# Mamba-2 scan and GELU layer on one core: the first decay scan widened, Y of two units in Gram banks, and a new hand order

## The chip, the cores and the metric

The kernel runs on one core of one Trainium2 chip. The metric is device time in microseconds, from one launch; the median of three runs stands for the kernel. TensorE (PE), VectorE (DVE), ScalarE (ACT), GpSimd (POOL) and SyncE (SP) each carry out their own instructions in program order and wait for each other through semaphores. SP and ACT also issue DMAs; such an issue holds up what stands behind it on that engine's queue.

## The reference, cut to what matters

```python
# x: (4, 8, 768, 32), a: (4, 8, 768), B and C: (4, 8, 768, 16); chunk-wise decayed linear attention
cum = np.cumsum(log(clip(a)))                  # per chunk
L = exp(cum_i - cum_j) * (i >= j)
M = (C_i . B_j) * L
y = M @ x + exp(cum) * (C @ state)
state = decay_full * state + sum_j decay_from_j * B_j x_j
# the heads are put side by side: 3072 tokens x 256
h = x @ w_in                                   # 256 -> 2048
out = gelu_tanh(h) @ w_out                     # 2048 -> 256
```

All inputs and the output are float32 in HBM; the kernel multiplies in bf16.

## The kernel before

The kernel uses chunks of 128 tokens: six chunks in each of four batches, 24 in all. Two chunks make a unit, so there are 12 units, three in each batch. A step has a name such as `Y.1` (the Y of unit 1) or `s1.0.6` (the first matrix product of unit 0, part 6), and one Python function `f_...` writes its instructions. The order of all steps is written out by hand in the string `ORDERED` (lines 17 to 68). The steps are written in that order, so each engine and each DMA queue works through its own part of it. A suffix `:A`, `:D`, `:P` or `:S` picks the engine for a step that can run on several (its `alt`), `@b` picks the PSUM bank, and `~51` puts in 51 blocks of idle matmuls on a zero tile (line 773).

**The scan.** In place of logarithms, a decay scan runs backwards over each chunk. `Rq` (line 371) scans the first four chunks of batch 0 for all batches' rows (128 partitions by 128); `R` (line 400) scans everything, 128 by 256. `tpq`, `tp2` and `tp6` (line 375) turn the results so that tokens are partitions; `recip0`, `recip1` and `recip` take reciprocals. B is multiplied by the decay (`mulb`, `mul1.0`, `mul.b.0`) and C by its reciprocal (`mulc`, `mul1.1`, `mul.b.1`). Batch 0 is done in two groups: chunks 0 to 3 (`bc0`, `tw`, `ew`) and chunks 4 and 5 (`load_bc1`, `mul1`, `T1`, `ce1`, `bh1`, `N1`, `bn1`). Batch 1 turns its B and C on TensorE (`T`, `E`, `F`, `N`, `bn`). Batches 2 and 3 write the scaled B and C to HBM scratch (`load_wr`, line 521), and read them back, with a DMA transpose (`load_tr`, line 527) and plainly (`load_bn`, line 533). In the names of these steps the last digit is 0 for B and 1 for C: `load_tr.2.0` brings the turned B of batch 2, which `G.6` needs.

```python
            wr = {i: add("S", load_wr, b, i, deps=[mul[i]]) for i in (1, 0)}
            tr = {1: add("S", load_tr, b, 1, deps=[wr[1], after]), 0: add("S", load_tr, b, 0, deps=[wr[0], Gn[last]])}
            bb = add("S", load_bn, b, deps=[wr[0], dn[last]])
...
        if alt:
            s.fn = lambda: fn(*args, {"A": "ACT", "D": "DVE", "P": "POOL", "S": "SP"}[s.eng])
        else:
            s.fn = lambda: fn(*args)
```

These lines (925 to 929 and 834 to 837) show that a `load_wr` step has no `alt`: its function takes no engine and always issues on SP.

**A unit.** `G` makes the Gram blocks in the PSUM tiles `ga` and `gb` (two banks each), `M` masks them into SBUF, `D` makes the state's increment, `S` adds it to the decayed state (line 752), `SP` spreads the state into a masked 128x256 tile (line 759), `Y` multiplies M by x and adds the state's part (lines 701 and 710), and `yev` copies Y to `xm` in SBUF. For units 0 and 1, `XX` and `XD` make x and the increment from one load of x (lines 601 and 611). From unit 4 on, two units are done together (`Yi`, `YI`, `yew`). Y of units 0 to 3 is made in `bank_y`.

**The GELU layer.** `s1` multiplies `xm` by `w_in` into a PSUM bank (lines 790 and 795), `gelu` on ScalarE moves it to SBUF (lines 801 and 804), `s2` multiplies by `w_out` (line 816), `oev` copies the result out of PSUM and `store` writes it. The four banks a, b, o, y are shared by these steps. The weights come as eight 512 KB loads (`load_wi`, `load_wo`) and are cast to bf16 by `wi` and `wo`; x comes by `load_x` (two DMAs for a unit) and is cast by `castx`.

## Time and profile before

| what | value |
| --- | --- |
| median of three runs | 116.5 us (115.69, 116.5, 119.59) |
| the profiled execution's own time | 115.84 us |
| its span, first to last instruction | 114.1 us |
| PE busy | 107.5 us (94%) |
| DVE, ACT, POOL busy | 68.1, 69.7, 24.7 us |
| moved by DMA | 15.99 MB in 43102 packets |
| granted TensorE clock | 1.000 |

The lines of the profile are in the prediction. Busy PE time counts matmuls whose modelled ends overlap, and it counts the idle matmuls on the zero tile too. The span lies 1.7 us below the execution's own time.

### The profile page before, as it was taken

How to read it: one execution, taken by the hardware profiler on the slowest of the kernel's cores; microseconds unless marked ns; L12 is line 12 of the kernel's file. 1: busy time of each engine (PE TensorE's matmuls, PEld its weight loads, DVE VectorE, ACT ScalarE, POOL GpSimd, SP SyncE). 2: the span in 40 equal slices, each digit the busy share in tenths (PEclk: the TensorE clock that was granted, in tenths of full speed). 3: DMA queues.
4: the chain of work that ended last, by engine and by line, in shares of the span. 5: the costliest groups of instructions: out<-in, count | busy, mean ns of one | idle time of the engine just before them, and what ended most of it. 6: DMA issues, size and time to landing. Idle time of an engine off the chain costs nothing.

```text
span 114.1 us, 3122 instructions
## 1 busy us (share of the span) xinstructions
PE 107.5 (94%) x1277; PEld 77.6 (68%) x1285; DVE 68.1 (60%) x136; ACT 69.7 (61%) x135; POOL 24.7 (22%) x53
## 2 busy tenths in 40 slices
PE   6998889999999999999999999999999999999990
PEld 2345566888879888665677765777657776777870
DVE  4789999999989597798509704658444411020110
ACT  3149688687673727479666778725865666654400
POOL 6635676736319000130200200000000000000000
PEclk9999999999999999999999999999999999999999
DMA  0999989989998768968777502220000023201032
GB/s 24 243 303 306 353 222 203 311 151 345 207 215 136 158 163 188 294 128 195 185 161 142 116 0 96 97 92 6 0 0 0 6 91 116 69 0 52 0 138 92
DMA packets 43102, 15.99 MB, mean 140 GB/s; under 512 B 36688, under 2 KB 41552, under 8 KB 43088
## 3 DMA queue, kind: packets, MB, share of 16 engines
q1 hardware_dynamic: 42896, 15.70, 54.9%
q8 instruction: 10, 0.16, 0.7%
q10 hardware_dynamic: 192, 0.09, 0.3%
q14 instruction: 4, 0.03, 0.1%
HBM read 11.07 MB, written 3.93 MB: 131 GB/s over the span
## 4 chain that ended last, share of the span: by engine, by line
PE 78%; SPq 9%; DMA 7%; ACT 1%; issue 1%; POOL 1%; DVE 0%; POOLq 0%
PE bank_o L816 19%; PE bank_y L816 16%; PE bank_b L795 10%; PE bank_a L795 7%; PE bank_b L790 5%; PE bank_a L790 4%; SPq L154 4%; PE bank_o L795 4%; DMA bcf<-in_B_dram 4%; DMA x_t<-in_x_dram 3%; PE bank_y L795 3%; SPq L194 3%; PE bank_b L816 2%; PE bank_a L816 2%; PE ga L637 1%; PE bank_y L721 1%
## 5 line engine op out<-in xcount | busy, mean ns | idle before, releaser
L816 PEld LDWEIGHTS <-gT 128*128 128x128 bf16 x384 | 37.1, 98 | 10.4 <-issue 0.6
L816 PE MATMUL bank_o<-w_out_sb,gT 128*128 128x256 bf16 x192 | 26.1, 273 | 0.0
L816 PE MATMUL bank_y<-w_out_sb,gT 128*128 128x256 bf16 x160 | 21.2, 273 | 0.1
L795 PEld LDWEIGHTS <-w_in_sb 128*128 128x128 bf16 x128 | 14.1, 114 | 7.7 <-issue 0.4
L804 ACT ACTIVATE gT<-bank_b 128x512 bf16<-128x512 f32 x25 | 14.9, 598 | 6.6 <-PE bank_b L795 6.1
L654 DVE TENSOR_TENSOR m<-ga,tri 128x1024 bf16<-128x1024 f32 x12 | 14.6, 1216 | 5.3 <-PE gb L637 5.3
L804 ACT ACTIVATE gT<-bank_a 128x512 bf16<-128x512 f32 x21 | 12.6, 599 | 6.6 <-PE bank_a L795 2.5
L790 PEld LDWEIGHTS <-w_in_sb 128*128 128x128 bf16 x128 | 13.6, 113 | 2.3 <-issue 1.5
L795 PE MATMUL bank_b<-xm,w_in_sb 128*128 128x512 bf16 x48 | 14.5, 380 | 0.2
L801 ACT ACTIVATE gT<-bank_b 128x512 bf16<-128x512 f32 x17 | 10.1, 596 | 6.8 <-PE bank_b L790 6.7
L654 DVE TENSOR_TENSOR m<-gb,tri 128x1024 bf16<-128x1024 f32 x11 | 13.4, 1216 | 0.1
L352 DVE COPY o_sb<-bank_y 128x256 f32<-128x256 f32 x5 | 2.1, 424 | 15.7 <-PE bank_y L816 13.7
L795 PE MATMUL bank_a<-xm,w_in_sb 128*128 128x512 bf16 x36 | 11.2, 380 | 0.1
L801 ACT ACTIVATE gT<-bank_a 128x512 bf16<-128x512 f32 x15 | 8.9, 595 | 2.7 <-PE bank_a L790 2.6
L790 PE MATMUL bank_b<-xm,w_in_sb 128*128 128x256 bf16 x68 | 10.3, 273 | 0.2 <-DVE s_new L752 0.2
L790 PE MATMUL bank_a<-xm,w_in_sb 128*128 128x256 bf16 x60 | 9.0, 272 | 0.9 <-ACT gT L801 0.4
L759 DVE SCALAR_TENSOR_TENSOR sp_new<-s_new,pend,bmask 128x256 bf16<-128x256 f32 x17 | 9.4, 568 | 0.3 <-DVE s_new L752 0.2
L773 PE MATMUL bank_y<-wz 128*128 128x512 bf16 (+2 forms) x21 | 7.6, 512 | 1.1 <-DVE warm L225 1.1
L352 DVE CAST xm<-bank_a 128x512 bf16<-128x512 f32 x4 | 2.8, 692 | 9.0 <-PE bank_a L734 9.0
L804 ACT ACTIVATE gT<-bank_o 128x512 bf16<-128x512 f32 x10 | 6.0, 596 | 2.4 <-PE bank_o L795 2.3
L510 POOL TENSOR_TENSOR bc<-bc_t,pt 128x768 bf16<-128x768 f32 x3 | 4.5, 1494 | 13.0 <-DMA bc_t<-in_C_dram 10.7
L348 ACT ACTIVATE xm<-bank_y 128x512 bf16<-128x512 f32 x8 | 4.8, 594 | 3.6 <-PE bank_a L734 3.1
(149 smaller groups left out, 131.8 us busy)
## 6 DMA issues: line engine op xcount, KB each, us to landing
out_dram<-o_sb SPq DMA_DIRECT2D x24, 128.0 KB, 1.8
x_t<-in_x_dram SPq DMA_DIRECT2D x20, 128.0 KB, 4.3
wf<-in_moe_w_in_dram SPq DMA_DIRECT2D x4, 512.0 KB, 7.6
wf<-in_moe_w_out_dram SPq DMA_DIRECT2D x4, 512.0 KB, 6.0
bc_t<-in_C_dram SPq DMA_DIRECT2D x3, 384.0 KB, 4.7
bc_t<-in_B_dram SPq DMA_DIRECT2D x3, 384.0 KB, 6.0
scr<-bc SPq DMA_DIRECT2D x4, 192.0 KB, 2.7
x_t<-in_x_dram SPq DMA_DIRECT2D x1, 512.0 KB, 4.5
```

The source lines that it names most:

```text
L154: nc.sync.dma_start(out=BC0[1][:, i], in_=(B, C)[i][0, :, c * Q:(c + n) * Q, :] .rearrange("h (p r) n -> p h (r n)", r=n))
L348: nc.scalar.activation(o, i, AF.Copy)
L352: nc.vector.tensor_copy(out=o, in_=i)
L510: (nc.gpsimd if eng == "POOL" else nc.vector).tensor_tensor(out=d["bc16"][:, i], in0=d["bc"].rearrange("p i h (r n) -> p i r h n", r=R6)[: ...
L654: nc.vector.tensor_tensor(out=m_of(u)[:, 2 * i:2 * i + 2].rearrange("p g k e t -> p (g k e) t"), in0=gx[i].rearrange("p g (k t) -> p (g k) ...
L759: nc.vector.scalar_tensor_tensor(out=sp_new.rearrange("p (g d) -> p g d", g=4), in0=(XN[0][:, H * D:H * D + 64] if gc == 0 else state[("s" ...
L773: nc.tensor.matmul(out=t[:, 0:m * 128], lhsT=wz, rhs=w3.to_broadcast([128, m, 128]), start=True, stop=True, skip_group_check=True)
L790: nc.tensor.matmul(out=hp[:, j * T:(j + 1) * T], lhsT=w_in_k[:, w, q, k], rhs=xm[:, w, u * T:(u + 1) * T], start=(w == 0), stop=(w == 1))
L795: nc.tensor.matmul(out=hp, lhsT=w_in_k[:, w, q, k], rhs=xm[:, w, u * T:u * T + PT], start=(w == 0), stop=(w == 1))
L801: nc.scalar.activation(gts[u][:, 2 * i:2 * i + 2], hp.rearrange("p (j t) -> p j t", j=2), AF.Gelu_apprx_tanh)
L804: nc.scalar.activation(gts[("p", u)][:, i], hp, AF.Gelu_apprx_tanh)
L816: nc.tensor.matmul(out=ops[gc], lhsT=gts[u][:, fi, k * Q:(k + 1) * Q], rhs=w_out_sb[:, fi, :], start=(fi == 0 and (u > 0 or k == 0)), stop ...
```

## The change

The diff does six things.

- `load_aq` now loads other rows: for batch 0 the 128 partitions hold chunks 0 to 5, so that the scan `Rq` serves chunks 4 and 5 too. `tp2` goes; `recip1` and `mul1` read what `tpq` made. `peq`, `ppq`, `pendq` and `m4` have six columns.
- `load_bc1` brings B and C of chunks 4 and 5 as 64 partitions with four tokens each (256 B runs) where it brought 128 partitions with two (128 B runs). `mul1`, `T1`, `ce1`, `bh1` follow that shape.
- Y of units 1 and 2 (`YG`) is made in `gb` instead of `bank_y`, its state part with 32x32 tiles, and for these units `SP` writes a 128x64 tile with one operand, on DVE or ACT.
- `pe` can run on POOL; the step `hold.4` goes.
- `XD` now comes before `XX`.
- The order from `mulb` on is another one, with other engines and banks for many steps.

```diff
+    YG = (1, 2)
...
-    BC0 = [const.tile([128, 2, H, n * N], FP32, name=f"bcf{g}") for g, (_, n) in enumerate(GR)]
+    BC0 = [const.tile([P4 * n, 2, H, R4 * N], FP32, name=f"bcf{g}") for g, (_, n) in enumerate(GR)]
...
-                          .rearrange("h (p r) n -> p h (r n)", r=n))
+                          .rearrange("h (p r) n -> p h (r n)", r=R4))
...
+            in_=bass.AP(tensor=a.tensor, offset=a.offset + i * Q, ap=[[R4 * Q, 32 // H], [S, H], [1, Q]]))
...
-    def f_tp2():
-        for k in range(4):
-            q, t = divmod(4 * Q + k * (Q // 2), QL)
-            turn(rt0[1][32 * k:32 * k + 32], r_t[32 * q:32 * q + 32, t:t + Q // 2], 2)
...
     def f_Y(u):
+        if u in YG:
+            for k, w, j in [(k, w, j) for k in range(2) for w in range(2) for j in range(4)]:
+                h = 4 * w + j
+                nc.tensor.matmul(out=gx[1][32 * j:32 * j + 32, w, k * Q:(k + 1) * Q],
+                                 lhsT=X16[u][:, k, 32 * h:32 * h + 32], rhs=MT[u][:, h // 2, k, h % 2],
+                                 start=(k == 0), stop=True, tile_position=(0, 32 * j), skip_group_check=True)
+            for k in range(2):
+                sp = state.pop(("sp", 2 * u + k - 1))
+                for h in range(H):
...
+                    nc.tensor.matmul(out=gx[1][32 * j:32 * j + 32, w, k * Q:(k + 1) * Q],
+                                     lhsT=sp[gs, 32 * e:32 * e + 32], rhs=ce_of(2 * u + k)[gs, e],
+                                     start=False, stop=True, tile_position=(32 * g, 32 * j), skip_group_check=True)
+            return
...
+    def f_SP(gc, eng):
+        if (gc + 1) // 2 in YG:
+            sp_new = st.tile([128, 64], BF16, name="sp_row")
...
-    hold = add("P", f_hold, 4, deps=[SPn[4]])
-    steps["mul.1.1"].deps.append(hold)
```

The new order, in the parts that the prediction speaks of (each line is cut out of the string):

```
recip0 c_m16 mulc.0 ~51 tw.1 ew.1.1:A mulc.1 tw.2 ew.0.1:A c_unp ew.1.2:A ~4 mulb tw.0 load_wi.1 ew.0.0:A
ew.0.2:A c_ends clip R tp6 G.0 peq ~4 ew.1.0:A x4.0:P x4.1:D M.0.0 pe:P GE.3 ppq XD.0 XX.0 ~4 GE.2 ME.3:P
pendq:A ME.2:D xn.1:A xn.0:D wi.0.0:A SP.0 S.0.0 S.0.1 load_wi.2 load_wi.3 Y.0 load_bc1.1 G.1 yev.0.0.2:A
...
load_bc1.0 wi.1.0:P gelu.0.0 wi.2.0:D SP.2:D wi.1.1:P s1.0.2@o s1.0.3@y gelu.0.2 wi.2.1:P s1.0.4@b
gelu.0.4 s1.0.5@o wi.3.0:P M.1.0 mul1.1:P Y.1 pp@a load_wo.0 gelu.0.3 load_x.2:S wi.3.1:D mul1.0:D
s1.0.6@y yev.1.0.2:A recip.1 gelu.0.5 gelu.0.6 T1.0 T1.1 wo.0.0:P bh1:D load_wo.2 s1.0.7@b N1 s1.1.0@y
...
D.4@a load_x.5:S SP.6 Y.3 s2.1.0.2 s2.1.0.3 castx.5.None:P load_wr.2.1:S load_x.6:A oev.2:A S.4.0
load_x.7:S yev.3.0.2:D S.4.1 SP.9 load_tr.2.1 s1.3.0@y s1.3.1@b s1.3.2@a gelu.3.0 gelu.3.2 s1.3.3@o
load_wr.2.0:A s2.1.1.0@y s2.1.1.1 M.4.1 s2.1.1.2 gelu.3.1 M.4.0 G.5 D.5@b S.5.0 gelu.3.3 s2.1.1.3 oev.3:A
SP.7 s1.3.4@b s1.3.5@o s1.3.6@a gelu.3.6 gelu.3.5 load_bn.2 SP.10 M.5.0 M.5.1 gelu.3.4 s2.2.0.0@y
load_tr.2.0 s2.2.0.1 F.2 s2.2.0.2 castx.6.None:D s2.2.0.3 oev.4:D s1.3.7@a castx.7.None:P gelu.3.7 SP.8
s2.2.1.0@o s2.2.1.1 s2.2.1.2 Yi.4@ya Yi.5 YI.4 YI.5 G.6 D.6@b D.7@y load_bc.3.0 s2.2.1.3 load_x.11:A
```

Before, the same stretch on SP's queue was: `load_x.5 load_x.6 load_wr.2.1 load_x.7 load_wr.2.0 load_tr.2.1 load_bn.2 load_tr.2.0`.

## The prediction

> **What bounds the kernel now.** I read first the page's head and its slices: how full TensorE is, and where it is not.

> ```profile
> span 114.1 us, 3122 instructions
> PE 107.5 (94%) x1277; PEld 77.6 (68%) x1285; DVE 68.1 (60%) x136; ACT 69.7 (61%) x135; POOL 24.7 (22%) x53
> ...
> PE   6998889999999999999999999999999999999990
> ...
> DMA  0999989989998768968777502220000023201032
> ```

> TensorE is full from the seventh slice (about 17 us) to the end; only the start has room, and there the DMA engines are full for the first 13 slices (37 us). Next the stages, by a view of four windows, cut at the points that the chain of waits gave below (us busy and instructions for PE, PEld, DVE, ACT and POOL; then clock, DMA share and GB/s).

> ```profile
> 12.40:20.35 7.95, 6.83 (x92) 5.15 (x93) 7.84 (x21) 6.39 (x13) 5.95 (x11) 1.00 0.99 242
> 20.35:31.50 11.15, 11.15 (x148) 9.75 (x148) 10.60 (x17) 7.98 (x15) 5.78 (x9) 1.00 0.99 253
> 31.50:45.60 14.10, 13.95 (x198) 11.96 (x201) 11.43 (x20) 8.07 (x17) 3.49 (x3) 1.00 0.83 171
> 45.60:111.10 65.50, 65.01 (x700) 45.70 (x708) 28.98 (x50) 40.50 (x79) 2.72 (x3) 1.00 0.34 87
> ```

> From 20.35 us on TensorE is busy 11.15 of 11.15, 13.95 of 14.10 and 65.01 of 65.50 us. In these stages nothing can be won but about 0.6 us; time can only be lost. In the first it is busy 6.83 of 7.95 us, and real idle time is more, since the modelled ends of matmuls overlap: nine `s1` steps at the 0.44 us that four matmuls take when nothing waits (eight take 0.89 in the chain below), and about 1.6 us of small work, leave some 2.3 us. DVE is busy 7.84 of 7.95 us there, and the DMA engines are at 0.99. The chain of waits says where that stage ends:

> ```profile
> 19.68 0.62 POOL x L350
> 20.35 0.21 PE bank_b L679 x4
> ...
> 31.47 0.89 PE bank_o L816 x8
> ```

> Until 20.35 the chain runs through the cast of x for unit 2 on POOL and `D.2`, which waits for it; from there it is TensorE alone. The step that ends at 32.36 (31.47 + 0.89) is `s2.0.1.3`. The changed order has done exactly the same `s1` and `s2` parts and units when it ends that step, so I use it as a milestone. The timeline shows the pace ahead of it:

> ```profile
> 8.83 1.20 DVE L654 TENSOR_TENSOR m<-ga,tri 128x1024 bf16<-128x1024 f32 x1
> ...
> 11.59 0.58 ACT L348 ACTIVATE xm<-bank_y 128x512 bf16<-128x512 f32 x1
> ...
> 15.04 1.17 POOL L350 CAST w_in_sb<-wf 128x512 bf16<-128x512 f32 x2 [0.20 <-DMA wf<-in_moe_w_in_dram]
> ...
> 15.59 0.60 ACT L801 ACTIVATE gT<-bank_a 128x512 bf16<-128x512 f32 x1 [0.20 <-PE bank_a L790]
> ...
> 16.72 0.60 PE L790 MATMUL bank_b<-xm,w_in_sb 128*128 128x256 bf16 x4
> 16.77 0.68 POOL L470 TENSOR_TENSOR bc0s<-bcf,rt 128x256 bf16<-128x256 f32 x1 [0.56 <-DMA bcf<-in_B_dram]
> ...
> 16.87 0.60 ACT L801 ACTIVATE gT<-bank_a 128x512 bf16<-128x512 f32 x1 [0.20 <-PE bank_a L790]
> ...
> 17.36 0.59 ACT L801 ACTIVATE gT<-bank_b 128x512 bf16<-128x512 f32 x1
> ...
> 18.76 0.60 PE L790 MATMUL bank_b<-xm,w_in_sb 128*128 128x256 bf16 x4
> ```

> `M.0.0` starts at 8.83, Y of unit 0 is copied at 11.59. The `s1` steps of unit 0 go round two banks, so each waits for the `gelu` two steps ahead: the `gelu` of bank a start 1.28 us apart (15.59, 16.87), 0.64 for one, while ScalarE can start one each 0.49 us (16.87, 17.36). `s1.0.6` is the row at 16.72. Then `s1.0.7` comes only at 18.76, since `T1`, `Y.1`, `pp` and `N1` stand in front of it and wait for B of chunks 4 and 5. The POOL rows show two landings, since both had waited for a DMA: `w_in` part 3 at 15.0, B of chunks 4 and 5 at 16.7.

> **The change part by part, the start.** The prices come from groups of instructions by shape (busy us and mean ns):

> ```profile
> L375 DVE STREAM_TRANSPOSE rt<-r_t 32x64 f32<-32x64 f32 x4 | 0.9, 238 | 0.1
> L362 DVE TENSOR_SCALAR ac<-a_t 128x256 f32<-128x256 f32 x1 | 0.3, 283 | 0.0
> L365 DVE TENSOR_TENSOR_SCAN r_t<-ac,ends 128x256 f32<-128x256 f32 x1 | 0.7, 692 | 0.1
> L375 DVE STREAM_TRANSPOSE rt<-r_t 128x192 f32<-128x192 f32 x1 | 0.5, 519 | 0.0
> L451 DVE TENSOR_TENSOR bc0s<-bcf,rt 128x512 bf16<-128x512 f32 x1 | 0.7, 691 | 0.4 <-DMA bcf<-in_B_dram 0.4
> L510 DVE TENSOR_TENSOR bc<-bc_t,rt 128x768 bf16<-128x768 f32 x2 | 1.9, 952 | 0.0
> L510 POOL TENSOR_TENSOR bc<-bc_t,rt 128x768 bf16<-128x768 f32 x1 | 1.7, 1681 | 0.0
> L759 DVE SCALAR_TENSOR_TENSOR sp_new<-s_new,pend,bmask 128x256 bf16<-128x256 f32 x17 | 9.4, 568 | 0.3 <-DVE s_new L752 0.2
> ```

> *Decay.* `tp2` goes (0.9 us of DVE) and `pe` goes to POOL. But `clip`, `R` and `tp6` (0.28, 0.69 and 0.52 us) now stand ahead of `M.0.0` on DVE; most of that lies in the wait for `G.0` and x. All six `ew` copies are on ACT, where DVE had two, so one more stands ahead of `G.0`: between 0 and the 0.58 us of the copy at 11.59, which is twice as wide; I take 0.3. With `ME.2` on DVE, Y of unit 0 is copied at about 12.0 rather than 11.59: **+0.4 us**.

> *`mul1` on half the partitions* is 512 elements wide instead of 256. On DVE that is the 0.69 us of `mulb` (line 451). On POOL, 256 elements took 0.68 and 768 took 1.68, so 1.1 to 1.2. They lie beside the `s1` steps of unit 0; if uncovered they cost 0.4 us each. The 64-column `SP` has a quarter of the elements of the 568 ns row, and takes between 0.14 and 0.57 us; I take 0.25. That frees 1.2 us of DVE or moves it to ACT, in a stage in which DVE is full. `load_bc1` has half as many packets. The two old loads took 1.7 us (15.0 to 16.7); the saving lies between 0 and half of that, I take 0.5 us for all later loads.

> *Y of units 1 and 2 in `gb`* has 32 matmuls of 128 columns as before: 0.45 us if four run side by side, as their column positions allow (eight of 256 columns take 0.89 in a row), and 1.1 if the new state part did not. I take no change, since TensorE has idle time around `Y.1`. Its worth is that `bank_y` is free: the `s1` steps of unit 0 go round three banks, so the pace is that of ScalarE, 0.5 us, not 0.64. Over the seven steps up to `Y.1` that is **-1.0 us**; it can't be more, because `w_in` part 3 lands at 15.0 whatever the order. `Y.1` stands ahead of `s1.0.6`, so the hole before `s1.0.7` shrinks by **0.4 us**. `s1.0.7` then starts at 17.8.

> *Up to the milestone.* `D.2` stands after four parts of unit 1, so it no longer waits for x (about 0.5 us of the time up to 20.35): **-0.5**. Against it, `mul.1.0` takes 1.68 us on POOL instead of 0.95 on DVE, behind a bc load that comes later by one weight load (512 KB at 253 GB/s is 2 us): `T.1.0` makes TensorE wait **+0.3**. Three `w_out` casts and `E.1.0` on ACT lie in the time that ACT has spare (it is busy 7.98 of 11.15 us).

> Sum: +0.4 - 1.0 - 0.4 - 0.5 + 0.3 = **-1.2 us** at the milestone. Bounds: -3.0 if TensorE had no hole at all after 12.4, +0.4 if only the later start stays.

> **The change, where the lead goes.** After the milestone the work on TensorE is the same, so the lead is kept only if nothing that comes by DMA is late. I followed SP's queue (start and length of each issue), one POOL row, and the landing times of the scratch transfers (min, median, max) and of the transposes:

> ```profile
> 26.54 2.71 SPq L168 DMA_DIRECT2D bc_t<-in_C_dram  x1
> ...
> 35.73 0.67 SPq L524 DMA_DIRECT2D scr<-bc  x1
> 36.45 2.26 SPq L175 DMA_DIRECT2D x_t<-in_x_dram  x2
> 38.81 0.89 SPq L524 DMA_DIRECT2D scr<-bc  x1
> 40.13 1.23 SPq L531 DMA_TRANSPOSE ch<-scr  x1
> 41.59 0.39 SPq L536 DMA_DIRECT2D bn<-scr  x1
> 42.03 1.23 SPq L531 DMA_TRANSPOSE bh<-scr  x1
> ```

> ```profile
> 34.15 1.49 POOL L510 TENSOR_TENSOR bc<-bc_t,pt 128x768 bf16<-128x768 f32 x1 [2.29 <-DVE s_new L752]
> ```

> ```profile
> DMA to landing us min/median/max: 2.1/2.8/4.4
> ```

> ```profile
> bh<-scr SPq DMA_TRANSPOSE x2, 3.1
> ```

> ```profile
> 45.60 0.29 PE L637 MATMUL ga<-ce,bh 32*64 32x256 bf16 x1
> ```

> Here `L510` at 34.15 is `mul.2.1`: its bc load, issued at 26.54, landed just then. It ends at 35.64, and SP writes C to scratch at 35.73. SP goes on to x for unit 7 and writes B to scratch at 38.81. At 40.13, when the first write has landed (4.4 us, the maximum), it issues C's transpose; at 41.59, when the second has landed, the plain reload; and at 42.03 B's transpose, which lands 3.1 us later at about 45.2. `G.6` (line 637) needs that and starts at 45.60, right behind `YI` on TensorE. So the old order met that load with 0.4 us to spare, and a lead of 1.2 us brings TensorE there 0.8 us too early, if the load comes as before.

> The new order moves `load_x.6` off SP to ACT, and puts the write of B behind the transpose of C. The mark `load_wr.2.0:A` changes nothing, because that step has no choice of engine and issues on SP. So: `mul.2.1` ends at 35.1 (35.64 less the 0.5 from `load_bc1`). The write lands between 2.1 and 4.4 us later. It now has only one unit's x ahead of it on SP's queue instead of two, so I take the 2.7 of the old second write: 37.8. C's transpose holds SP for 1.23: 39.1. Then B's write, again 2.7: 41.85; the reload is issued with 0.05 to spare, and B's transpose 0.44 after it, as before: 42.35, landed 45.45. **`G.6` starts at 45.5 instead of 45.60: -0.1 us is left of the lead**, and TensorE stands idle for 1.1 us ahead of it. `D.6`, `D.7`, `s2.2.1.3` and all later parts queue behind `G.6`.

> [...]

> **ACT's DMA issues.** `load_x.6`, `.11` and `.10` on ACT are two issues each: 0.8 us by the unhindered 0.39 at 41.59, and up to 2.3 us by the SP row of `load_x.7` (36.45). They stand where ACT waits for TensorE anyway (ACT is busy 8.07 of 14.10 us). I take 0; uncovered, about 1 us.

> **Batch 3** has the same pattern: `load_wr.3.0` holds up SP ahead of `load_bc.3.1`. Its transposes are needed by `G.9`, and by the same steps I count some 6 us to spare. I take 0.

> Sum against the execution's own time: 115.84 - 0.1 = **115.7 us**; the median shown is 0.7 above that execution.

> **The rivals.**

> *The lead is kept.* If B's write lands at the minimum of 2.1 us, and C's at 2.1 too, G.6's load lands at 44.2, and TensorE, which arrives at 44.4, does not wait: 115.84 - 1.2 = 114.6 us, and down to 113.0 if the start comes near its bound of -3.0. For it: fewer packets, and one unit's x less on SP's queue. Against it: the DMA share of 0.83 up to 45.6, and landings of 2.7 to 4.4 in just that stretch.

> *Slower, by the order on SP.* If either write lands in 4.4 us, as the old one did, B's transpose is 1.7 us later, lands at 47.15, and `G.6` starts at 47.2 rather than 45.60: 115.84 + 1.6 = 117.4. It decides as soon as B's transpose is issued after 42.4. For it: nothing overlaps any more, C's write, C's transpose and B's write follow one another. Against it: SP's queue is less full by then.

> *The change doesn't do what it says at the start.* Products on POOL slow DVE, and there is no lead.

> ```profile
> 34.19 1.73 DVE L759 SCALAR_TENSOR_TENSOR sp_new<-s_new,pend,bmask 128x256 bf16<-128x256 f32 x1
> ```

> This `SP` took 1.73 us while POOL multiplied, against 0.57 in the mean: 1.2 us for one instruction. If that strikes at `F.1`, which `G.3` needs, the lead is 0. TensorE then reaches `G.6` at 45.6, its load is there, and the time is 115.84 to 116.3, I take 116.0. [...]

> **How the numbers follow.** Lead spent at `G.6`, 115.7 us: 0.43 (own range 115.0 to 116.4). Lead kept, 114.6: 0.28. Slower on SP, 117.4: 0.16. No lead, 116.0: 0.13. The range of 8 in 10 goes from 114.0 to 117.6: it takes in both landing bounds and leaves out a start that gains over 1.8 us and a stall of over 1.8. The chances go by 2%, about what a measurement of this kernel can tell from no change: below 114.2 (of 116.5) lies about half of "lead kept", the half with the better start, 0.15; above 118.8 lies the part of "slower" that has a second stall, for `G.9` or for x, and a little of the unforeseen, 0.10; the rest, 0.75, is within 2%.

> **What would show it.** Right: `s2.0.1.3` ends near 31.2, the issue of B's transpose of batch 2 lies near 42.4 and behind C's, `G.6` at 45.5 has idle time before it of about 1 us, and TensorE is full from there. Wrong: `G.6` without idle time and earlier than 45 (lead kept), `G.6` at 47 (slower), or `s2.0.1.3` at 32 or later (no lead). What would make it wrong altogether is a hole of TensorE after 46 us, or a start in which the first `s1` step of unit 0 comes after 13.5.

## The result, and the profile after

The changed kernel takes **119.7 us** (median of 119.11, 119.48, 119.87 and 122.64), the kernel before 116.4 in the same series. The ratio is 1.029, with a 95% interval of 1.023 to 1.035: slower, where 115.7 us within 114.0 to 117.6 had been forecast. The profiled execution took 119.87 us, with a span of 118.2 instead of 114.1. (The ratio leaves disturbed executions out, here 122.64 and one of 119.59 of the kernel before; so do the medians and ratios below, by which the changed kernel takes 119.5.)

The page's head and slices, to be held against those of before:

```profile
span 118.2 us, 3112 instructions
PE 110.8 (94%) x1276; PEld 77.9 (66%) x1284; DVE 67.5 (57%) x132; ACT 69.2 (59%) x136; POOL 25.9 (22%) x52
...
PE   6977699999999999999999999999999999999990
...
PEclk9999755999999999999999999999999999999999
```

TensorE has 3.3 us more busy time with one instruction less, and the clock row has a dent in its fifth to seventh slice (12 to 21 us) that the kernel before does not have. The stages again, cut at the steps of this kernel (PE, PEld, DVE, ACT, POOL busy; then clock, DMA share, GB/s):

```profile
13.50:20.00 6.50, 6.50 (x75) 3.99 (x72) 5.39 (x14) 3.28 (x8) 3.74 (x6) 0.50 1.07 239
...
20.50:35.50 15.00, 15.00 (x219) 12.40 (x219) 9.20 (x20) 12.89 (x25) 7.51 (x8) 1.00 1.07 244
35.50:49.30 13.80, 13.57 (x191) 11.31 (x192) 11.67 (x19) 6.86 (x14) 3.21 (x4) 1.00 0.98 164
49.30:115.20 65.90, 65.24 (x700) 45.73 (x708) 30.73 (x52) 40.02 (x76) 3.47 (x3) 1.00 0.33 76
```

TensorE is granted half its clock in the whole of the first window; in windows of 0.2 us the fall lasts from 13.4 to 20.3 us, 6.8 us. From 20.5 us on it is full, as before. The `s1` steps of unit 0 lie in the dent; `s1.0.0`, `s1.0.1`, `s1.0.5`, `s1.0.6` and the first step of unit 1 in the timeline:

```profile
15.30 1.04 PE L816 MATMUL bank_b<-xm,w_in_sb 128*128 128x256 bf16 x4
16.14 1.06 PE L816 MATMUL bank_y<-xm,w_in_sb 128*128 128x256 bf16 x4
...
19.55 0.95 PE L816 MATMUL bank_o<-xm,w_in_sb 128*128 128x256 bf16 x4
21.26 0.60 PE L816 MATMUL bank_y<-xm,w_in_sb 128*128 128x256 bf16 x4
...
22.78 0.49 PE L816 MATMUL bank_y<-xm,w_in_sb 128*128 128x256 bf16 x3
```

Four matmuls take 0.84 us to the next start at half clock, where the kernel before needed 0.64 on two banks. The first step comes at 15.30 instead of 12.43, the milestone (end of `s2.0.1.3`) at 35.57 instead of 32.36, `G.6` at 49.31 instead of 45.60. So 2.9 of the 4.1 us between the two spans are there before the first `s1` step, 3.2 at the milestone; 0.9 are lost behind it.

The start is late from its first DMA. Rows of before (SP's queue, ACT's queue, VectorE):

```profile
0.82 0.86 SPq L158 DMA_DIRECT2D aq_t<-in_a_dram  x2
...
0.81 0.89 ACTq L158 DMA_DIRECT2D aq_t<-in_a_dram  x2
...
3.32 0.23 DVE L362 TENSOR_SCALAR acq<-aq_t 128x128 f32<-128x128 f32 x1 [1.17 <-DMA aq_t<-in_a_dram]
```

and of after:

```profile
0.81 1.55 SPq L161 DMA_DIRECT2D aq_t<-in_a_dram  x2
...
0.82 1.91 ACTq L161 DMA_DIRECT2D aq_t<-in_a_dram  x2
...
4.55 0.24 DVE L368 TENSOR_SCALAR acq<-aq_t 128x128 f32<-128x128 f32 x1 [1.12 <-DMA aq_t<-in_a_dram]
```

`load_aq` with its new pattern of rows takes 1.55 and 1.91 us to issue instead of 0.86 and 0.89; `clipq`, the head of the whole chain, starts 1.2 us later. Further on TensorE stands still, as its waits from 8 to 16 us show (waits of before in that stretch: none over 0.3):

```profile
PE bank_y L724 <- DVE x L358: 1.0, 1, 1.0
PE ga L642 <- ACT ce L354: 0.7, 1, 0.7
PE bank_o L462 <- DVE bc0s L453: 0.5, 1, 0.5
```

The first of them, ahead of `Y.0`, is where the kernel before had the idle matmuls `~17`. The new order has no such blocks there.

### The profile page after: what moved, and what is told of

Its sections match the earlier page's. It is cut to its first block, busy times and chain, and to the rows that moved or that the text cites. A ratio compares the mean times of both kernels' runs of the same rounds, so it can differ in the third digit from the quotient of the medians.

```text
span 118.2 us, 3112 instructions
## 1 busy us (share of the span) xinstructions
PE 110.8 (94%) x1276; PEld 77.9 (66%) x1284; DVE 67.5 (57%) x132; ACT 69.2 (59%) x136; POOL 25.9 (22%) x52
## 5 line engine op out<-in xcount | busy, mean ns | idle before, releaser
L821 PEld LDWEIGHTS <-w_in_sb 128*128 128x128 bf16 x128 | 14.1, 114 | 7.6 <-issue 0.2
L830 ACT ACTIVATE gT<-bank_a 128x512 bf16<-128x512 f32 x22 | 13.1, 597 | 6.0 <-PE bank_a L821 3.6
L816 PEld LDWEIGHTS <-w_in_sb 128*128 128x128 bf16 x128 | 14.3, 120 | 2.6 <-issue 0.6
L830 ACT ACTIVATE gT<-bank_b 128x512 bf16<-128x512 f32 x22 | 13.1, 597 | 4.0 <-PE bank_b L821 4.0
L652 DVE TENSOR_TENSOR m<-gb,tri 128x1024 bf16<-128x1024 f32 x11 | 13.4, 1218 | 1.5 <-PE gb L635 1.2
L821 PE MATMUL bank_b<-xm,w_in_sb 128*128 128x512 bf16 x43 | 12.9, 379 | 0.1
L830 ACT ACTIVATE gT<-bank_o 128x512 bf16<-128x512 f32 x12 | 7.2, 596 | 2.6 <-PE bank_o L821 2.6
L799 PE MATMUL bank_y<-wz 128*128 128x512 bf16 (+1 forms) x16 | 6.8, 579 | 1.1 <-DVE warm L229 1.1
L358 DVE COPY o_sb<-bank_o 128x256 f32<-128x256 f32 x4 | 1.7, 425 | 9.7 <-ACT o_sb L354 7.0
L821 PE MATMUL bank_o<-xm,w_in_sb 128*128 128x512 bf16 x24 | 7.2, 380 | 0.1
L827 ACT ACTIVATE gT<-bank_b 128x512 bf16<-128x512 f32 x10 | 6.0, 597 | 1.8 <-PE bank_b L816 1.8
L816 PE MATMUL bank_b<-xm,w_in_sb 128*128 128x256 bf16 x40 | 7.0, 303 | 0.0
L830 ACT ACTIVATE gT<-bank_y 128x512 bf16<-128x512 f32 x8 | 4.8, 599 | 3.7 <-PE bank_y L821 3.0
L354 ACT ACTIVATE xm<-bank_y 128x512 bf16<-128x512 f32 x5 | 3.0, 597 | 6.5 <-PE bank_a L748 5.3
L827 ACT ACTIVATE gT<-bank_y 128x512 bf16<-128x512 f32 x9 | 5.4, 600 | 2.0 <-PE bank_y L816 1.9
```

The source lines that it names most:

```text
L354: nc.scalar.activation(o, i, AF.Copy)
L358: nc.vector.tensor_copy(out=o, in_=i)
L652: nc.vector.tensor_tensor(out=m_of(u)[:, 2 * i:2 * i + 2].rearrange("p g k e t -> p (g k e) t"), in0=gx[i].rearrange("p g (k t) -> p (g k) ...
L799: nc.tensor.matmul(out=t[:, 0:m * 128], lhsT=wz, rhs=w3.to_broadcast([128, m, 128]), start=True, stop=True, skip_group_check=True)
L816: nc.tensor.matmul(out=hp[:, j * T:(j + 1) * T], lhsT=w_in_k[:, w, q, k], rhs=xm[:, w, u * T:(u + 1) * T], start=(w == 0), stop=(w == 1))
L821: nc.tensor.matmul(out=hp, lhsT=w_in_k[:, w, q, k], rhs=xm[:, w, u * T:u * T + PT], start=(w == 0), stop=(w == 1))
```

## The experiments

Theory after these rows: three things together make the start late, the pattern of `load_aq` (1 us), the half clock that follows from a TensorE left idle (1 to 2 us), and the new order itself. Rival: the new order alone, with both others as mere by-products. Later experiments asked why a mended start did not bring the forecast gain.

**Before, without the fill.** Only the fill ahead of `Y.0` is taken out of the old order.

```diff
-... load_wi.2 SP.0 ~17 Y.0 wi.0.1:A ...
+... load_wi.2 SP.0 Y.0 wi.0.1:A ...
```

> The kernel before, without the 17 blocks of idle matmuls ahead of Y of unit 0; nothing else is changed. Theory 'clock' (TensorE does too little between 10 and 13.5 us, and is granted half its clock for some 7 us): the granted clock shows a stage at 0.5 of about 6.8 us from 12 to 14 us on, and the time rises by 2 to 4 us. Theory 'late start' (the slower load of a alone shifts everything): the clock stays 1.0 and the time stays within 0.5 us.

Measured: 116.54 us against 116.28, ratio 1.002 (0.998 to 1.006). Single executions differ by their mean clock: 115.9 to 116.6 at 0.98 to 1.00, 117.1 and 117.4 at 0.97. The profiled one, 117.4, is of the latter; first a row of before, then two of `e1`:

```profile
7.00:11.00 4.00, 3.39 (x66) 1.86 (x69) 3.76 (x12) 3.51 (x10) 2.75 (x13) 1.00 1.03 312
```

```profile
7.00:11.00 4.00, 2.39 (x62) 1.50 (x63) 3.63 (x11) 2.86 (x8) 2.66 (x13) 0.98 1.04 339
11.00:17.50 6.50, 6.50 (x90) 3.61 (x91) 5.33 (x15) 3.93 (x8) 3.99 (x8) 0.50 0.99 278
```

With the fill TensorE is busy 3.39 of these 4.00 us and the clock stays at 1.00; without it the clock falls, in six of nine executions, and the long fall (two of the nine) costs about 1 us, less than the 2 to 4 forecast.

**Before, with the new `load_aq`.** One function exchanged.

```diff
-in_=a_rows(i * Q, Q)
+in_=bass.AP(tensor=a.tensor, offset=a.offset + i * Q, ap=[[R4 * Q, 32 // H], [S, H], [1, Q]])
```

> The kernel before, with the new access pattern of load_aq alone (the rows that this kernel uses are the same). 'Late start': the two issues on SP take 1.5 us instead of 0.86, the first decay scan and all later steps come 1.0 us later, and the time rises by about 1.0 us, to 116.8 to 117.5. 'Clock': the pattern alone shifts the start but the idle matmuls stay, the clock stays 1.0, and the time rises by 0.3 to 1.0 us at most, since part of the shift is hidden by the loads; if the gap that it opens is enough, a stage at half clock appears and the time rises by 3 us or more.

Measured: 117.12 us, ratio 1.008 (1.005 to 1.012), clock 1.00 in nine of ten executions. Every step of the start is 1.0 us later (`s1.0.0` 13.41, `s1.0.7` 19.76), and 0.8 of it reaches the end. This cost stands by itself.

**After, with a fill; with a plain load; with both.** `e3` puts `~20` ahead of `Y.0`. `e4` loads the rows that are used as six DMAs of two levels. `e5` has that load and three fills.

```diff
 # e4, e5: load_aq
+for p, n, t in ((0, H, i * Q), (H, 32 - H, (R4 + i) * Q)):     # for i = 0, 1; i = 2, 3 as before the change
+    e.dma_start(out=aq_t[32 * i + p:32 * i + p + n],
+                in_=bass.AP(tensor=a.tensor, offset=a.offset + t, ap=[[S, n], [1, Q]]))
 # e5 (of the fills e3 has the last only)
-... tp6 G.0 ... ppq XD.0 ... load_wi.3 Y.0 ...
+... tp6 ~8 G.0 ... ppq ~8 XD.0 ... load_wi.3 ~20 Y.0 ...
```

> The changed kernel with 20 blocks of idle matmuls (1.1 us) put back ahead of Y of unit 0, where TensorE waits 1.0 to 1.4 us anyway. 'Clock': no stage at half clock, the first s1 steps take 0.44 to 0.5 us instead of 0.86, and the time falls from 119.5 to 116.5 to 117.5. 'Late start': the clock may rise, but the s1 steps wait for weights and gelu as before, and the time falls by less than 1 us.

> The changed kernel, with the first decay scan's rows loaded by six DMAs of plain two-dimensional patterns instead of four of three dimensions (the rows used are the same, the unused ones differ). 'Late start': each issue takes 0.4 us, the scan starts 0.7 to 1.0 us earlier, and the time falls by 0.7 to 1.0 us. 'Clock': the start moves, but the half clock stays, and the time falls by 0 to 1 us; if the shorter gap ahead of Y of unit 0 keeps the clock, it falls by 3 us.

> The changed kernel with both mends: plain loads of a in six DMAs, and idle matmuls put back in three places (8 blocks ahead of G.0, 8 ahead of XD.0, 20 ahead of Y of unit 0). So far a run of the changed kernel at full clock took 117.9, one at half clock for 7 us 119.4; the slow load pattern alone cost 0.8. Theory 'sum of three' (clock 1.5, load pattern 0.8, order 0.9 us): the clock is 1.0 and the time is 117.0 to 117.4, still about 0.9 above the kernel before. Rival 'clock and load are all': 116.3 or less. Rival 'order is most': 118 or more at clock 1.0.

Measured: `e3` 118.9 us, ratio 1.017 (1.007 to 1.026), and 117.93 in the one of its three executions at full clock; `e4` 119.4, 1.025 (1.020 to 1.029), no better than the changed kernel; `e5` 118.6 and 118.9 in the two executions at full clock (the two others took 122.8 at 0.98 to 0.99). The clock differs with what TensorE has to do from 8 us on. These are the rows of `e4` and then of `e5`, for 8 to 13 us and the stretch behind it:

```profile
8.00:13.00 5.00, 3.20 (x80) 1.73 (x84) 4.86 (x11) 2.88 (x8) 2.62 (x6) 0.83 1.02 332
13.00:20.00 7.00, 7.00 (x111) 4.50 (x108) 5.48 (x13) 4.24 (x10) 3.83 (x6) 0.63 0.94 217
```

```profile
8.00:13.00 5.00, 4.43 (x89) 2.06 (x91) 4.63 (x11) 2.85 (x8) 3.00 (x6) 1.00 0.98 331
13.00:20.00 7.00, 6.67 (x126) 4.91 (x126) 6.26 (x14) 5.73 (x12) 3.56 (x6) 1.00 1.03 217
```

In `e4` the clock falls at 11.3 us, inside the first window, and each matmul takes longer from there (from `s1.0.0` to `s1.0.1`, four matmuls, 0.84 us, where eight take 0.89 at full clock), so its 3.20 us busy is no fair count; in the 3.4 us ahead of the fall (the length of the shortest fall, `e3`'s) TensorE was busy 2.21 us, in `e5` in the same stretch 2.85.

At the milestone the steps read: after 35.57, `e4` 34.50, `e5` 32.98, before 32.36. By these profiles the load has 1.1 of the 3.2 us there, the half clock 1.5 and the rest of the change 0.6. The shares are rough: `e8` and `e9` below have `e5`'s order up to the milestone and reach it at 33.79 and 33.81, and `e12` has the changed kernel's and reaches it at 34.72, so one profile is good to some 0.8 us. That the load and the clock cost time, against the rival, rests on `e2` and on the long falls of `e1`. The end did not follow the milestone: `e4`'s gain is not seen there at all, and `e5` has won 2.6 us at the milestone and only 1.5 at the span (116.7).

**The decay chain moved back.** `e6` is `e5` with a shorter chain ahead of `G.0`.

```diff
-... c_ends clip R tp6 ~8 G.0 ... M.0.0 pe:P GE.3 ... S.0.1 load_wi.2 ... wi.2.1:P s1.0.4@b ... yev.1.0.2:A recip.1
+... c_ends ~8 G.0 ... M.0.0 GE.3 ... S.0.1 clip R load_wi.2 ... wi.2.1:P pe:P s1.0.4@b ... yev.1.0.2:A tp6 recip.1
```

> As the run with both mends, and clip, R, tp6 and pe stand behind the first states again instead of ahead of M of unit 0 on DVE and of ME on POOL. 'Sum of three', with the order's 0.9 us lost in that DVE chain ahead of Y of unit 0: the first s1 step comes 0.7 to 1.2 us earlier and the time falls to 116.0 to 116.5. Rival (the order's loss lies in XX and G behind Y of unit 0, or later than the first s1 step): the first s1 step moves, the time by less than 0.3 us.

Measured: 118.6 us. `s1.0.0` is 0.4 us earlier (13.67), `s1.1.0` 0.2 later (20.19), and nothing is won.

**All in the old order.** `e7`: the code of the changed kernel with the plain load, steps in the order of before.

> The changed code (scan for chunks 4 and 5, 64-partition mul1, Y of units 1 and 2 in Gram banks, 64-column states, plain loads of a) in the order of the kernel before, less tp2 and hold.4 and with XD ahead of XX. 'The order is at fault': 116.0 to 116.6, as before or 0.3 better. Rival 'the code itself is slower' (512-element products on POOL, 32x32 state matmuls): 117 or more.

Measured: 118.2 us once at full clock, 120.7 to 122.2 in three executions at 0.97, among them the profiled one, in which TensorE waited 1.7 us for `pe`. This does not decide between the code and the order.

**The later holes.** `e5` had two, by its waits from 38 to 60 us, and this is the VectorE row behind the first:

```profile
PE ga L646 <- DVE m L656: 0.8, 1, 0.8
PE bank_y L825 <- DVE o_sb L362: 0.7, 1, 0.7
...
36.79 1.49 DVE L789 SCALAR_TENSOR_TENSOR sp_new<-s_new,pend,bmask 128x256 bf16<-128x256 f32 x1
```

`G.5` waited for `M.4.0`, which stood behind `SP.9`, an instruction of 0.5 us that took 1.49 beside the product `mul.2.0` on POOL; `oev.6` waited for an output buffer whose store stood behind `load_x.9`. `e8` mends both; `e9` also moves B's write, the prediction's step.

```diff
 # e8, e9
-S.4.1 SP.9 load_tr.2.1 ... M.4.1 s2.1.1.2 gelu.3.1 M.4.0 G.5 ... load_x.9:S store.0 s1.4.3@b store.1
+S.4.1 M.4.1 M.4.0 SP.9 load_tr.2.1 ... s2.1.1.2 gelu.3.1 G.5 ... store.0 s1.4.3@b store.1 load_x.9:S
 # e9
-load_tr.2.1 ... load_wr.2.0:A ... load_bn.2 ... load_tr.2.0
+load_wr.2.0:A load_tr.2.1 load_bn.2 load_tr.2.0
```

> The changed kernel with old load_aq and 36 fills in the start had its milestone (end of s2.0.1.3) only some 0.6 us behind the kernel before, and still took 118.6 to 118.9 us at full clock. Its TensorE had two holes later: 0.77 us ahead of G.5 (M.4.1 and M.4.0 stood on VectorE behind SP.9, which took 1.49 us beside mul.2.0 on GpSimd) and 0.70 us ahead of a step of unit 4 in bank y (oev.6 waited until an output buffer had been stored; store.0 stood on SP behind load_x.9). This kernel moves M.4.1 and M.4.0 ahead of SP.9 and load_x.9 behind store.1. Theory A (the two holes are the whole later loss): both go, 117.2 us. Theory B (the prediction's step: G.6 cannot come before load_tr.2.0 has landed, and that is issued behind load_wr.2.0, which stands behind load_tr.2.1): G.6 stays at about 47.1 us, only the second hole goes, 118.0 us. Theory C (the holes move on and nothing is won): 118.7 us.

> As e8_a_mid, and load_wr.2.0 issued ahead of load_tr.2.1, with load_bn.2 and load_tr.2.0 right behind it. Theory A: as e8_a_mid within 0.2 us, 117.2. Theory B: G.6 comes at about 46.3 us instead of 47.1 and the kernel takes 117.2 against 118.0 of e8_a_mid. Theory C: 118.7.

Measured: 118.3 us (117.84 and 118.76) and 118.06, ratio of the second 1.016 (1.007 to 1.025). Both holes are gone, and half a microsecond of the expected 1.5 is won. A new wait of 0.65 us for `SP.6` ahead of `Y.3` stood in `e8`'s profile, none after 30 us in `e9`'s. `G.6` came right behind `YI` in both; nothing shows it waiting for its load, so theory B's mechanism is not confirmed by `e9`'s gain.

**The same later mends without the early ones.** `e12` is the changed kernel with the mends of `e9` alone.

> The changed kernel with only the later mends of e9_a_mid_sp (M.4.1 and M.4.0 ahead of SP.9, load_wr.2.0 ahead of load_tr.2.1 with load_bn.2 and load_tr.2.0 behind it, load_x.9 behind store.1); its late start is left as it is. Theory A (in the changed kernel the later queue stalls are covered by the late start, its TensorE idles only 0.23 us at 38 to 40 us): 119.3 to 119.7 us, at most 0.4 less than the changed kernel. Theory B (they cost there too, as the prediction's step at G.6 has it): 118.2 to 118.8 us.

Measured: 119.7 us, ratio 1.026 (1.019 to 1.033), as without them (119.5). With the late start these holes were not what cost time.

**The old start.** `e10` is `e9` with the order and engines of before up to the third `gelu` (lines 18 to 23 of the old order), without the three fills of `e5`, with the old `~17`. `e11` and `e13` go on from there.

```diff
 # e11 on e10, e13 too
-gelu.0.2 tp6 pe:P ... load_bc1.0 wi.2.0:D ... load_wr.3.0:A ... mul.3.1:P s1.4.12@b load_x.8:S
+gelu.0.2 wi.2.0:P tp6 pe:P ... load_bc1.0 ... load_wr.3.0:A load_x.8:S ... mul.3.1:P s1.4.12@b
 # e13 on e11
-~4 G.0 ... pendq XD.0
+~4 ~8 G.0 ... pendq ~8 XD.0
```

> As e9_a_mid_sp, and its start up to the third gelu of unit 0 in the order and on the engines of the kernel before (with ~17 ahead of Y.0, without the added fills). If the new order of the start (x4.0 and ME.3 on GpSimd beside VectorE, G.1 and XX.1 ahead of s1.0.0) is what is left of the lateness at the front, s1.0.0 comes at 12.4 to 12.8 us instead of 14.1, and the kernel takes 115.8 to 116.4 us. If the later start lies in the larger first scan itself, s1.0.0 stays at 13.7 or later and the time within 0.3 us of e9_a_mid_sp. If moving it lets recip1, pe and tp6 fall behind on VectorE, a hole opens ahead of Y.1 or T1.0 as in e7_a_oldorder and the time is 118 or more.

> e10_a_hybrid started the first s1 step at 12.56 us as the kernel before does (12.43), and kept two holes: 1.4 us ahead of s1.0.4, which waited for the cast wi.2.0 behind M.1.1 and SP.1 on VectorE, and 0.5 us ahead of D.8, which waited for castx.8, because load_x.8 was issued at 53.7 us. Here wi.2.0 goes to GpSimd right behind the third gelu, and load_x.8 ahead of load_bc.3.1. Theory A (the change's core, three banks for s1 and Y of units 1 and 2 in Gram banks, does win about 1 us at the milestone once its start is not late): s2.0.1.3 ends at 31.5 to 32.0 us against 32.36 before, and the kernel takes 115.6 to 116.4 us. Theory B (the core wins nothing): the milestone stays at 32.4 or later, 116.6 to 117.4 us. Theory C (the load moved ahead makes another wait, of bc.3.1 and mul.3.1): the milestone moves and the time does not, 117.5 us.

> e11_a_hybrid2 with ~8 ahead of G.0 and ~8 ahead of XD.0. Nine of e11_a_hybrid2's twelve executions ran at a mean clock of 0.995 or more and took 116.53 to 117.24 us, two at 0.985 took 118.1 and 118.2, and its profiled one, in which the first x4 cast came 2.3 us late and left TensorE empty, ran at 0.971 and took 120.2. Theory A (the half clock follows from emptiness of TensorE in the start, and the core of the change wins about 1 us at the milestone): every execution at 0.995 or more, s2.0.1.3 ends at 31.4 to 32.0 us against 32.36 before, 116.3 to 116.9 us. Theory B (the core wins nothing): the milestone comes at 32.4 or later at full clock.

Measured: 117.96 us, ratio 1.012 (1.008 to 1.016); 116.8, 1.0065 (1.003 to 1.010); 116.96, 1.006 (1.002 to 1.010). In `e10` the first `s1` step is as early as before (12.56), so the late start was the new order, not the wider scan. The waits of `e10` name what ate it:

```profile
PE bank_b L819 <- DVE w_in_sb L361: 1.4, 1, 1.4
PE bank_b L680 <- DVE x L361: 0.5, 1, 0.5
```

`e11` removed both, which brought 1.2 us; it is the best version of the change, and it does not beat the kernel before. In all, the plain load, the fills and the later mends brought 1.4 us at the end (119.5 to 118.06), the old start with its two mends 1.3 (to 116.8), and 0.5 us against the kernel before (116.3) are left. The profiled execution of `e11` ran into the half clock (120.2 us), after a wait of 2.3 us for the cast of x. In `e13` every execution ran at 0.995 or more. The profile of `e13` shows what the core of the change does at full clock from a start almost as early as before (12.81). TensorE, then VectorE:

```profile
15.91 0.60 PE L819 MATMUL bank_o<-xm,w_in_sb 128*128 128x256 bf16 x4
17.09 0.41 PE L690 MATMUL gb<-m,x 128*32 128x128 bf16 x16 [0.58 <-DVE m L655]
...
17.92 0.60 PE L819 MATMUL bank_y<-xm,w_in_sb 128*128 128x256 bf16 x4
19.11 0.29 PE L482 MATMUL ga<-ident,bc0s 64*128 64x64 bf16 x4 [0.59 <-DVE bc0s L474]
```

```profile
15.82 1.22 DVE L655 TENSOR_TENSOR m<-ga,tri 128x1024 bf16<-128x1024 f32 x1
...
18.36 0.68 DVE L474 TENSOR_TENSOR bc0s<-bcf,rt 64x512 bf16<-64x512 f32 x1 [0.58 <-DMA bcf<-in_B_dram]
```

The `s1` steps run ahead on three banks: from `s1.0.0` to `s1.0.5` 3.10 us instead of 3.80 (in `e5`, which starts 1.6 us later than before, 2.72). Then `Y.1` waits for `M.1.0`, and `T1.0` for the product of B, whose load landed about 18.3 us; the kernel before starts that product at 16.77. The lead is gone at `s1.1.0` (20.04, before 19.20).

**Taking those two waits away.** `e14` is `e13` with another order on VectorE and `load_bc1` ahead of `load_wi.3`. `e15` is `e13` with one part of the change undone: chunks 4 and 5 are served by the main scan again.

```diff
 # e14
-gelu.0.2 wi.2.0:P tp6 pe:P load_wi.3 load_bc1.1 recip1 SP.1:A M.1.1 S.1.1 SP.3:D load_bc1.0 SP.2:D ... M.1.0
+gelu.0.2 load_bc1.1 load_bc1.0 load_wi.3 M.1.1 SP.1:A S.1.1 wi.2.0:P M.1.0 SP.3:D SP.2:D tp6 pe:P recip1 ...
 # e15: load_bc1, tp2, recip1, mul1, T1, ce1, bh1 as in the kernel before, and
-wi.1.0 wi.2.1 ... wi.2.0:P tp6 pe:P ... recip.1
+wi.1.0 tp2 wi.2.1 ... wi.2.0:P pe:P ... tp6 recip.1
```

> In e13_a_hybrid3 the s1 steps on three banks did run ahead (s1.0.5 at 15.91 us, before 16.23), and the lead was lost in two waits right behind: Y.1 stood 0.58 us for M.1.0, which ran on VectorE behind tp6, recip1, M.1.1, S.1.1 and two SP rows, and T1.0 stood 0.59 us for the product mul1.0, whose load_bc1.0 landed at 18.3 us. Here M.1.0 follows M.1.1 at once, tp6, pe and recip1 come behind, and load_bc1.1 and load_bc1.0 are issued ahead of load_wi.3. Theory A (the two waits are what eats the lead of three banks and of the Gram-bank Y): Y.1 at 16.5 us instead of 17.09, T1.0 at 18.3 instead of 19.11, the end of s2.0.1.3 at 31.8 to 32.1 instead of 32.83, 116.0 to 116.4 us. Theory B (VectorE itself is full from 13.4 to 18 us: what is moved back there comes late, and the next wait, for pe or recip1, takes the place of the old one): T1.0 stays at 18.9 or later, 116.8 to 117.3 us.

> e13_a_hybrid3 with chunks 4 and 5 served by the main scan again: load_bc1 with 128 partitions of 256 values, tp2, recip1, mul1, T1, ce1 and bh1 as in the kernel before; tp6 stands ahead of recip.1. In five profiles with the new load at full clock (s1.0.0 between 12.56 and 14.17 us) T1.0 came at 18.76 to 19.11 us and the first s1 step of unit 1 at 19.99 to 20.8, however early the start was: the second product ran at 17.9 to 18.4 us, behind the landing of load_bc1.0, which the kernel before has at 16.77. Theory A (the new load and product of chunks 4 and 5 pin T1.0, and eat what the three banks win): the load lands before 17.4 us, T1.0 comes before 18.4, the end of s2.0.1.3 before 32.4, 116.0 to 116.4 us. Theory B (T1.0 is late for VectorE, which now has tp2 with 0.99 us more): T1.0 stays at 18.8 or later, 116.8 to 117.4 us.

Measured: `e14` 117.89 us at full clock in the profiled execution, 119.6 to 121.7 at 0.97 to 0.99 in the others: the weights now came late instead, and TensorE waited 0.85 and 0.59 us for `wi` casts. `e15` 117.6 us (116.46 in the profiled one), ratio 1.013 (1.007 to 1.018). With the old load the B product ran at 17.75 and `T1.0` at 18.82, but `M.1.0` came later, and `Y.1` waited 0.94 us for it. Ahead of `M.1.0` on VectorE stand the two 64-column `SP`; here is their row in `e13` and then in `e15`, with what POOL did beside the second:

```profile
15.49 0.42 DVE L784 TENSOR_SCALAR sp_row<-s_new,pendq 128x64 bf16<-128x64 f32 x2
```

```profile
15.21 1.16 DVE L791 TENSOR_SCALAR sp_row<-s_new,pendq 128x64 bf16<-128x64 f32 x2
...
15.69 0.62 POOL L481 TENSOR_TENSOR bc0s<-bcf,pt 128x256 bf16<-128x256 f32 x1
```

They took 0.7 us more in `e15`, beside a cast and this product on POOL, which stood idle then in `e13`. Theory A fails in both, theory B is nearer: in these two runs each wait that was taken away at 13 to 18 us had another behind it. VectorE and the DMA engines have little to spare in that stage, as a window of `e13` shows:

```profile
13.00:18.00 5.00, 4.12 (x67) 3.19 (x66) 4.51 (x9) 3.64 (x9) 3.77 (x8) 1.00 1.16 266
```

VectorE is busy 4.51 of 5.00 us, beside its wait of 0.58 for B's load, and the DMA share is 1.16.

The profiles of all side by side, start of three steps, end of `s2.0.1.3`, and what is left from there to the end of the span (us):

| kernel | `s1.0.0` | `s1.1.0` | end of `s2.0.1.3` | `G.6` | from `s2.0.1.3` to the end |
| --- | --- | --- | --- | --- | --- |
| before | 12.43 | 19.20 | 32.36 | 45.60 | 81.7 |
| after | 15.30 | 22.78 | 35.57 | 49.31 | 82.6 |
| e4 plain load | 14.81 | 21.51 | 34.50 | 47.94 | 83.1 |
| e5 and fills | 14.06 | 19.99 | 32.98 | 47.14 | 83.7 |
| e9 and later mends | 13.95 | 20.47 | 33.81 | 47.15 | 82.4 |
| e10 and old start | 12.56 | 19.94 | 32.95 | 46.28 | 82.7 |
| e13 and its mends | 12.81 | 20.04 | 32.83 | 46.16 | 82.2 |
| e15 and old bc1 | 12.56 | 19.90 | 32.69 | 46.02 | 82.0 |

Open: why single executions of one kernel at full clock spread by up to 1.4 us (`e15`: 116.46 to 117.87), and what makes the last column 0.3 to 0.7 us longer than before even where TensorE has no wait (`e9`, `e13`).

## Why the prediction was wrong, point by point

The step that failed first is the start: priced at +0.4 us, it was 2.9 us late at the first `s1` step, so that no lead was left to spend at `G.6`.

- **What it left out was larger than all it counted.** `load_aq` is listed in the change, and no term was made for it: +0.8 us alone (`e2`), about 1.1 at the milestone here. That the new order lacks the idle matmuls of `~17` was not priced either. The prediction read the clock as 1.000 in every window and did not ask what kept it there: about 1.5 us at the milestone and 0.7 at the end (`e4` to `e5`).
- **The term +0.4 for a later start** was mis-sized. With load and clock mended `s1.0.0` still came 1.6 us late (`e5`, 14.06), and the old order of the start took that away (`e10`, 12.56). What that is worth at the milestone is not settled: `e10` reaches it at 32.95, `e9`, on which it builds, at 33.81, and `e5`, with the late start too, at 32.98.
- **The term -1.0 for three banks** is right in kind and in size: -0.7 from `s1.0.0` to `s1.0.5` in `e13`, -1.1 in `e5`, where 0.7 of the 1.0 had been forecast for these five distances.
- **The term -0.4, `Y.1` ahead of `s1.0.6`,** failed. `Y.1` there waits for `M.1.0` on VectorE, and holds up `s1.0.6` behind it: 17.92 against 16.72. From `s1.0.5` to `s1.0.7` it takes 3.53 us in `e13` (2.62 in `e5`) against 2.53 before, and `s1.0.7` starts at 19.44, not at the 17.8 forecast. The prediction had the number for it, VectorE busy 7.84 of 7.95 us, and then let TensorE's steps run ahead of VectorE's.
- **The saving of 0.5 for `load_bc1`** did not come at the load itself. The two issues hold SP for 0.73 and 0.64 us instead of 0.47 and 4.21 (`e13`, before), but B, issued 0.8 us later, landed at about 18.3 us, and its product started at 18.36 instead of 16.77. With the old pattern in the same order (`e15`) the product ran at 17.75 without waiting for a DMA. What the new pattern and what the order of the queue has of this delay stays open.
- **The terms -0.5 and +0.3 from unit 1 to the milestone** hold as a sum, within the scatter: from `s1.1.0` to the end of `s2.0.1.3` it takes 13.16 us before, 12.79 after and in `e13`, 13.34 in `e9`; -0.4 to +0.2 against a forecast of -0.2. A wait for `T.1.0`, the +0.3, is not among the waits of the changed kernel.
- **The lead spent at `G.6`** was never put to the test, because no version had a lead, and `G.6` followed `YI` without idle time (49.31 in the changed kernel). But SP's chain can be held against the forecast; these are its rows in the changed kernel, and the landing of the transposes of B:

```profile
35.26 0.79 SPq L525 DMA_DIRECT2D scr<-bc  x1
...
37.84 1.24 SPq L532 DMA_TRANSPOSE ch<-scr  x1
39.18 0.51 SPq L525 DMA_DIRECT2D scr<-bc  x1
42.91 0.37 SPq L537 DMA_DIRECT2D bn<-scr  x1
43.33 1.23 SPq L532 DMA_TRANSPOSE bh<-scr  x1
```

```profile
DMA to landing us min/median/max: 3.7/3.7/3.7
```

C's write (35.26), its transpose (37.84) and B's write (39.18) came within 0.2 us of the forecast 35.1, 37.8 and 39.1. B's write then took 3.7 us and not the 2.7 taken over from the old second write, and B's transpose 3.7 and not 3.1, so that it landed at 47.0 instead of 45.45. A TensorE with the lead would have waited until then if these times had stayed: that is the rival "slower, by the order on SP" (47.15), not the main forecast. That a lead is lost later was true of `e5`, at two other places: an `SP` of 1.49 us on VectorE ahead of `M.4.1`, and a store behind a load.

- **The sign that would make it wrong altogether**, a first `s1` step after 13.5 us, is what came: 15.30. No rival had it: "no lead" stopped at 116.0, and for a time above 118.8 the prediction gave 0.10, most of it to a second stall, for `G.9` or x. What "no lead" builds on, rows of VectorE that are slow beside a product on POOL, did show, but at other steps than `F.1`: 1.49 us for `SP.9` in `e5`, against 0.48 for the same shape at 34.55, and 1.16 for two rows in `e15`, against 0.42 in `e13`.

## What to carry to other kernels

Price every line of a diff that lies on the first chain, the small loads too: here a new pattern for the same bytes took 1.55 and 1.91 us to issue on the two queues instead of 0.86 and 0.89, and all of the start was 1.0 us later by that (`e2`). Ask of idle work in an order what it keeps up before it is dropped; here it kept TensorE's clock (without it the clock fell in six of nine executions of `e1`, with it in none of 18 of the kernel before). And where the profile says that an engine is full in a stage, a faster neighbour may only move the wait, as in `e14` and `e15` (VectorE busy 4.51 of 5.00 us in `e13`): follow the full engine's queue, not TensorE's, to the next place where the two meet.

## What the runs showed of the hardware

```profile
10.03:13.43 3.40, 2.16 (x67) 1.20 (x66) 3.30 (x7) 1.72 (x5) 2.25 (x6) 1.00 0.99 339
```

```profile
10.03:13.43 3.40, 3.15 (x81) 1.74 (x81) 3.05 (x11) 3.07 (x9) 2.02 (x4) 1.00 1.04 369
```

Ahead of the falls of `e1` (at 10.8 us), `e3` and `e4` (both at 11.3) TensorE was busy 2.10, 2.34 and 2.21 us of such a stretch; in the kernel before and in `e5`, whose clock stayed at 1.00, the same stretches hold 2.80 to 3.15 and 2.85 to 3.40. That is no limit on every stretch of 3.4 us: in `e10` TensorE was busy only 1.87 us from 15.0 to 18.4, and the clock stayed at 1.00; what sets the two cases apart no run shows. Nor was there one long gap: in the changed kernel the longest ahead of the fall was 1.0 us, and two of 0.7 and 0.5 stood further back. That idle time in the start brings the fall is shown by `e1`, whose only change is the missing fill: six of nine executions fell, and none of the 18 of the kernel before beside them, whose mean clocks are all 0.996 or more. In the profiles of after, `e1`, `e3` and `e4` a fall lasted 3.4 us (`e3`) or 6.8 (the three others).

The two issues of `load_aq` on SP took 1.55 us with three levels in the source pattern (changed kernel) and 0.86 with two (kernel before), for the same 16 KB each.
